# One PSUM pool of eight banks, and attention scores taken 512 keys at a time, in a fused sketch-attention and expert-attention kernel

## The chip, the core and the metric

The kernel runs on one core of a Trainium2 chip. The metric is device time in microseconds, the median of several executions. A core has a matrix engine (TensorE, PE in the profile; its weight loads are a row of their own, PEld), a vector engine (VectorE, DVE), an activation engine (ScalarE, ACT), a general one (GpSimd, POOL) and a queue for transfers (SyncE, SP). Matrix products land in PSUM, here used as eight banks of 128 partitions by 512 fp32 values; VectorE or ScalarE read them out from there.

## What is computed

Two blocks, one after the other. The first is an attention with a polynomial sketch: queries and keys (4 batches, 4 heads, 1088 positions, 32 values) become 64 features each, and the output is a ratio of two products with sums over all keys. Its output x, 1088 by 128 for each batch, goes through four "experts", each an ordinary causal attention of width 64; a gate picks two of four experts for each position. In short (cut):

```
for e in range(E):
    q = x @ wq[e]; k = x @ wk[e]; v = x @ wv[e]
    scores = scale * (q @ k.transpose(0, 2, 1))
    scores = np.where(causal, -1000000000.0, scores)
    scores = scores - scores.max(-1, keepdims=True)
    a = np.exp(scores)
    a /= a.sum(-1, keepdims=True) + 1e-09
    ye = a @ v @ wo[e]
    for kk in range(K):
        mask = topk[:, :, kk] == e
        out += mask[..., None] * w[:, :, kk:kk + 1] * ye
```

The change concerns the path from scores to a.

## The kernel before, in words

**Tiling.** Queries and keys are cut into tiles of 128 positions: i or j = 0 to 7, and a last tile of 64 (i = 8). Experts go in two groups g of two (e = 0, 1); the two sit in partitions 0 to 63 and 64 to 127 of qk and are multiplied side by side. Since the attention is causal, query tile i needs n = 128 i + 128 keys.

**The steps for one query tile and group.** `scores` (line 400) multiplies qk by qk into a tile sc (line 412), at most 512 keys an instruction. `soften` (393) lets VectorE add the mask, negate, store into an SBUF tile a, and keep the running minimum of the negated scores in mx (395); this is called a *take* below. ScalarE then computes the exponential of a in place with mx as bias and sums it into z (398). `turns_of` (469) transposes a on TensorE, tile by tile, into tp (477), which `evacuate` (67) copies into aT: every third copy goes to VectorE (70), the others to ScalarE (72). `values` (546) multiplies aT by v into av (552). `gates` (494) makes the weight rb from z (497 to 501); TensorE transposes it into the second half of the av tile (507), ScalarE copies it (509), and VectorE multiplies av by it into yT (557). That product empties the bank of av. `output` (614) multiplies yT by wo into po, which is copied and stored.

`scores_first` (421) does query tiles 0 and 1 together, `scores_last` (441) the last 64 queries of both groups: first the 64 diagonal keys into two tiles ext, then 1024 keys into sc. There VectorE takes ext first (through 395), then the 1024 keys in one instruction (464) that has the minimum of the ext take as its starting value, so the minimum of both comes out in mx; one exponential over all 1088 follows (466).

**PSUM.** Two pools. ps_sc (56) has two slots of two banks: an sc tile of 1024 keys of one expert, or of two experts by 512. ps_tp (57) has four slots of one bank for everything else: tp, av, po, ext, and the tiles of `prepare` (206), which makes qk, v and the gates of the next batch (kps and qps, the sketch; tq, num, tx, qk, vg). A tile may be written when the last reader of the bank's previous tile is done; such waits are put in when the program is built. Which slot a tile gets is also decided then.

**Order.** TensorE's instructions run in the order in which they are written (the block from 627 on). For each unit of work: `make` the scores of one query tile; multiply the values of groups that are ready; for a unit of kind G make the scores of the second query tile; then a row of jobs, transposes of the scores made before, mixed by `spend` (518) with pieces of `prepare` for the next batch (queued in `fill`). A batch has eight units: Q (tiles 0, 1), two of kind P (tiles 2, 3), four of kind G (tiles 4 to 7), L (the last 64). In the last batch there is no next one to prepare; units are split into kinds A and B. The other engines work in the order in which their instructions were scheduled at build time. Loads of the next batch are issued on SP in `begin_rest` (236), stores in `output` (624).

Of the kernel before, what the change touches and what calls it, by code (L numbers as in the profile page):

```python
# [10 lines left out]
F32 = mybir.dt.float32  # L11
BF16 = mybir.dt.bfloat16
I32 = mybir.dt.int32
ALU = mybir.AluOpType
ACTF = mybir.ActivationFunctionType
# [4 lines left out]
def kernel(  # L20
# [20 lines left out]
    nc = tc.nc  # L41
    B, H, S, D = q.shape
# [7 lines left out]
    NG = E // 2  # L50
    scale = 1.0 / math.sqrt(HD)
# [1 line left out]
    cp = ctx.enter_context(tc.tile_pool(name="const", bufs=1))  # L53
    p2 = ctx.enter_context(tc.tile_pool(name="p2", bufs=2))
    p4 = ctx.enter_context(tc.tile_pool(name="p4", bufs=4))
    ps_sc = ctx.enter_context(tc.tile_pool(name="ps_sc", bufs=2, space=bass.MemoryType.PSUM))
    ps_tp = ctx.enter_context(tc.tile_pool(name="ps_tp", bufs=4, space=bass.MemoryType.PSUM))

    def const(name, shape, dt=F32):
        return cp.tile(shape, dt, name=name, tag=name)  # L60
# [6 lines left out]
    def evacuate(out_, in_):  # L67
        turn[0] += 1
        if turn[0] % 3 == 0:
            nc.vector.tensor_copy(out_, in_)  # L70
        else:
            nc.scalar.copy(out_, in_)  # L72


    kin = const("kin", [128, S])
# [41 lines left out]
    with tc.issue_after(landing.ins):  # L117
        for x, w in enumerate((wq, wk)):
            nc.sync.dma_start(out=wqk[:, x], in_=w.rearrange("e p d -> p e d"))
        nc.sync.dma_start(  # L120
            out=wvg[:, 0 : E * HD].rearrange("p (e d) -> p e d", e=E), in_=wv.rearrange("e p d -> p e d"))
# [63 lines left out]
    mask = const("mask", [128, 1024], BF16)  # L185
# [20 lines left out]
    def prepare(b):  # L206
# [4 lines left out]
        gw = p2.tile([128, NJ, E], F32, tag="gw", name=f"gw{b}")  # L211
        gw8 = p2.tile([128, 2], F32, tag="gw8", name=f"gw8{b}")
        n = NJ - 1

        def bank(name):
            return ps_tp.tile([128, 512], F32, tag="tp", name=name)

        abS = {}
        fps = {}
# [170 lines left out]
        return (qk, vt, gw, gw8), ahead, mid, late  # L390


    def soften(a, src, msk, mx, z, most=3e38):

        nc.vector.tensor_tensor_reduce(out=a, in0=src, in1=msk, scale=-1.0, scalar=most,  # L395
                                       op0=ALU.add, op1=ALU.min, accum_out=mx)
        if z is not None:
            nc.scalar.activation(out=a, in_=a, func=ACTF.Exp, bias=mx, scale=-1.0, accum_out=z)  # L398

    def scores(b, i, g, qk, z):  # L400

        n = 128 * i + 128
        if n <= 512:
            t = ps_sc.tile([128, 2, 512], F32, tag="sc", name=f"sc{b}_{i}_{g}")
            sc = [t[:, e, :] for e in range(2)]
        else:
            sc = [ps_sc.tile([128, 1024], F32, tag="sc", name=f"sc{b}_{i}_{g}_{e}") for e in range(2)]
        for c0 in range(0, n, 512):
            c1 = min(c0 + 512, n)
            for e in range(2):  # L410
                rows = slice(64 * e, 64 * e + 64)
                nc.tensor.matmul(sc[e][:, c0:c1], qk[rows, g, 128 * i : 128 * i + 128], qk[rows, NG + g, c0:c1],  # L412
                                 start=True, stop=True)
        mx = p4.tile([128, 2], F32, tag="mx", name=f"mx{b}_{i}_{g}")
        width, tag, bufs = (512, "as", 8) if n <= 512 else (S, "a", 4)
        ats = [p4.tile([128, width], F32, tag=tag, name=f"a{b}_{i}_{g}_{e}", bufs=bufs) for e in range(2)]
        for e in range(2):
            soften(ats[e][:, 0:n], sc[e][:, 0:n], mask[:, 1024 - n :], mx[:, e : e + 1], z[:, e : e + 1])
        return ats

    def scores_first(b, qk, zs):

        made = [[[], []] for _ in range(NG)]
        for g in range(NG):
            t = ps_sc.tile([128, 2, 512], F32, tag="sc", name=f"sc{b}_0_{g}")
            for i in range(2):
                for e in range(2):
                    rows = slice(64 * e, 64 * e + 64)
                    nc.tensor.matmul(t[:, e, 128 * i : 256 * i + 128], qk[rows, g, 128 * i : 128 * i + 128],  # L429
                                     qk[rows, NG + g, 0 : 128 * i + 128], start=True, stop=True)  # L430
            mx = p4.tile([128, 2, 2], F32, tag="mx0", name=f"mx{b}_0_{g}")
            a = [p4.tile([128, 512], F32, tag="as", name=f"a{b}_0_{g}_{e}", bufs=8) for e in range(2)]
            for i in range(2):
                for e in range(2):
                    n, dst = 128 * i + 128, a[e][:, 128 * i : 256 * i + 128]
                    soften(dst, t[:, e, 128 * i : 256 * i + 128], mask[:, 1024 - n :], mx[:, i, e : e + 1],
                           zs[g][:, i, e : e + 1])
                    made[g][i].append(dst)
        return made

    def scores_last(b, qk, z):

        sc = [ps_sc.tile([128, 1024], F32, tag="sc", name=f"sc{b}_8_{e}") for e in range(2)]
        ext = [ps_tp.tile([128, 512], F32, tag="tp", name=f"ext{b}_{e}")[:, 0:64] for e in range(2)]

        def some(dst, e, c0, c1):
            rows = slice(64 * e, 64 * e + 64)
            for g in range(NG):
                nc.tensor.matmul(dst[64 * g : 64 * g + 64], qk[rows, g, 1024:], qk[rows, NG + g, c0:c1],  # L449
                                 start=True, stop=True)  # L450

        for e in range(2):
            some(ext[e], e, 1024, S)
        for c in range(0, 1024, 512):
            for e in range(2):
                some(sc[e][:, c : c + 512], e, c, c + 512)
        mx = p4.tile([128, 4], F32, tag="mx8", name=f"mx{b}_8")
        ats = [p4.tile([128, S], F32, tag="a", name=f"a{b}_8_{e}") for e in range(2)]
        for e in range(2):
            soften(ats[e][:, 1024:], ext[e], mask_last, mx[:, 2 + e : 3 + e], None)  # L460
        for e in range(2):

            most = mx[:, e : e + 1]
            nc.vector.tensor_tensor_reduce(out=ats[e][:, 0:1024], in0=sc[e], in1=mask[:, 0:1].to_broadcast([128, 1024]), scale=-1.0,
                                           scalar=mx[:, 2 + e : 3 + e], op0=ALU.add, op1=ALU.min, accum_out=most)
            nc.scalar.activation(out=ats[e], in_=ats[e], func=ACTF.Exp, bias=most, scale=-1.0, accum_out=z[:, e : e + 1])
        return ats

    def turns_of(name, i, ats, aT, q0):

        def some(e0, e1, j0, j1):
            tp = ps_tp.tile([128, 512], F32, tag="tp", name=f"tp{name}_{e0}_{j0}")
            nk, nj = size(j0), j1 - j0
            for e in range(e0, e1):
                for j in range(j0, j1):
                    x = 128 * (nj * (e - e0) + j - j0)
                    nc.tensor.transpose(tp[0:nk, x : x + 128], ats[e][:, 128 * j : 128 * j + nk], ident)  # L477
            evacuate(aT[0:nk, e0:e1, j0:j1, q0 : q0 + 128],
                     tp[0:nk, 0 : 128 * nj * (e1 - e0)].rearrange("p (e j s) -> p e j s", e=e1 - e0, j=nj))

        n = min(i + 1, NJ - 1)
        if n <= 2:
            cuts = [(0, 2, 0, n)]
        elif n <= 4:
            cuts = [(0, 1, 0, n), (1, 2, 0, n)]
        elif n <= 6:
            cuts = [(0, 1, 0, 4), (0, 2, 4, n), (1, 2, 0, 4)]
        else:
            cuts = [(0, 1, 0, 4), (0, 1, 4, n), (1, 2, 0, 4), (1, 2, 4, n)]
        if i == NJ - 1:  # L490
            cuts.append((0, 2, n, NJ))
        return [lambda c=c: some(*c) for c in cuts]
# [36 lines left out]
    def units(b, qk, vt, gw, gw8):  # L529
# [5 lines left out]
        for p in range((NJ - 1) // 2) if b < B - 1 else (1, 3, 2, 0):  # L535
# [3 lines left out]
            for g in range(NG):  # L539
# [4 lines left out]
                name = f"{b}_{p}_{g}"  # L544

                def values(p=p, g=g, aT=aT, yT=yT, name=name):
                    av = ps_tp.tile([128, 512], F32, tag="tp", name=f"av{name}")
                    for j in range(2 * p + 2):
                        lo = 128 * max(0, j - 2 * p)
                        for e in range(2):  # L550
                            c = HD * (2 * g + e)
                            nc.tensor.matmul(av[HD * e : HD * e + HD, lo:256], vt[:, j, c : c + HD],  # L552
                                             aT[:, e, j, lo:256], start=(j == 0), stop=(j == 2 * p + 1))

                    def finish(to_gate):
                        rs = to_gate(av[:, 256:])
                        nc.vector.tensor_tensor(out=yT[:, g], in0=av[:, 0:256], in1=rs, op=ALU.mult)  # L557
                        return [lambda: output(b, p, yT)] if g == NG - 1 else []

                    return finish  # L560
# [26 lines left out]
    def last_unit(b, qk, vt, gw8):  # L587
# [3 lines left out]
        yT = p2.tile([128, NG, 256], F32, tag="yT", name=f"yT{b}_8")  # L591

        def values():
            av = ps_tp.tile([128, 512], F32, tag="tp", name=f"av{b}_8")
            for g in range(NG):
                for j in range(NJ):
                    m = size(j)
# [15 lines left out]

    def output(b, p, yT):
        nq, n = (128, 2) if p < NJ // 2 else (64, 1)
        po = ps_tp.tile([128, 512], F32, tag="tp", name=f"po{b}_{p}")
        for x in range(n):
            for g in range(NG):
                nc.tensor.matmul(po[0:nq, DM * x : DM * x + DM], yT[:, g, 128 * x : 128 * x + nq], wo_sb[:, g],  # L619
# [6 lines left out]

    with tc.manual_schedule(engines={mybir.EngineType.PE}):

        warm = ps_tp.tile([128, 512], F32, tag="tp", name="warm")
        for _ in range(16):  # L630
            nc.tensor.matmul(warm[:, 0:128], idle, idle, start=True, stop=True)
        now, ahead, _, own = prepare(0)
# [103 lines left out]
```

## Time and profile before

The median of 3 runs is 398.3 us (398.27 to 398.81). The profiled execution took 398.61 us by the device's count, and its span in the profile is 396.8 us. The granted clock of TensorE is 1.0 of full speed all through.

| what | us or share | where it is read |
|---|---|---|
| span | 396.8 | top of the page |
| GpSimd busy | 58.7 (15%) | engine row |
| score matmuls, lines 412 / 429 / 449 | 320 / 64 / 64 records | groups of one tile |
| takes of scores (line 395) | 90.2 us, 128 times | costliest groups |
| exponentials (line 398) | 98.1 us, 128 times | costliest groups |
| transposes of a (line 477) | 90.1 us, 648 records | costliest groups |
| wait of takes for score matmuls | 62.1 us, 33 times | waits |
| wait of exponentials for takes | 59.2 us, 38 times | waits |
| chain that ended last: PE / DVE / ACT | 72% / 15% / 9% | chain of waits |

One fp32 matmul leaves two records. A row of the costliest groups gives the line, the engine and its operation, output<-input by name and shape, the count, busy time and mean, and behind the bar the idle time of the engine before these instructions and what ended it. Busy time of TensorE includes the modelled ends of pipelined matmuls. An idle time of VectorE or ScalarE costs nothing unless TensorE waits for what comes behind it.

### The profile page before, as it was taken

Reading aid. Unit: us, or ns where it says so; the run is one execution under the profiler, and the core shown is the slowest. Engines: PE = TensorE matmul, PEld = TensorE weight load, DVE = VectorE, ACT = ScalarE, POOL = GpSimd, SP = SyncE. Lnnn points to the kernel's source line nnn. Section 1 sums busy time; section 2 is a strip of 40 time slices with the busy share of each in tenths; the row PEclk is TensorE's granted clock in tenths of the full one; section 3 lists DMA queues with packets and bytes.
Section 4 is the critical chain, followed back from the end, with each engine's and each line's share of the span. In section 5 each row is a group of like instructions: output and inputs, shape, how many; then the busy total and the mean of one; then the engine's idle time right before and its main releaser. Section 6 shows DMA issues by size and latency. Waiting matters only on the chain.

```text
span 396.8 us, 8017 instructions
## 1 busy us (share of the span) xinstructions
PE 373.2 (94%) x3152; PEld 265.4 (67%) x3152; DVE 234.6 (59%) x661; ACT 226.5 (57%) x550; POOL 58.7 (15%) x87
## 2 busy tenths in 40 slices
PE   8898999999999999999999999999999999999995
PEld 7764687667665776767664767766756475666673
DVE  6867866555548675366456564555655844745551
ACT  2236666555666656456475656754665565656582
POOL 3400461000001740000000541000000010000010
PEclk9999999999999999999999999999999999999999
DMA  7705022000000000000000000000000000000000
GB/s 192 200 2 170 16 98 71 2 1 15 13 2 0 15 2 5 15 0 15 1 15 0 2 13 7 13 2 0 15 13 2 1 16 6 0 15 2 15 4 26
DMA packets 11349, 9.95 MB, mean 25 GB/s; under 512 B 3632, under 2 KB 10288, under 8 KB 11312
## 3 DMA queue, kind: packets, MB, share of 16 engines
q1 hardware_dynamic: 11296, 9.44, 8.6%
q8 instruction: 24, 0.39, 0.4%
q14 instruction: 13, 0.11, 0.1%
q10 hardware_dynamic: 16, 0.00, 0.0%
HBM read 7.22 MB, written 2.23 MB: 24 GB/s over the span
## 4 chain that ended last, share of the span: by engine, by line
PE 72%; DVE 15%; ACT 9%; issue 2%; DMA 2%; SPq 0%; ACTq 0%; DVEq 0%
PE av L552 16%; PE sc L412 15%; PE tp L477 14%; DVE a L395 7%; ACT a L398 7%; PE qk L326 5%; PE vg L338 3%; PE num L300 3%; PE po L619 3%; PE av L600 3%; PE sc L449 2%; DMA qin<-in_q_dram 2%; DVE qT L223 1%; PE sc L429 1%; PE qps L251 1%
## 5 line engine op out<-in xcount | busy, mean ns | idle before, releaser
L398 ACT ACTIVATE a<-a,mx 128x256 f32<-128x256 f32 (+7 forms) x128 | 98.1, 767 | 59.6 <-DVE mx L395 59.2
L395 DVE CUSTOM_DVE_ANT_0 a<-sc,mask 128x256 f32<-128x256 f32 (+7 forms) x128 | 90.2, 754 | 64.1 <-PE sc L412 62.1
L477 PE MATMUL tp<-ident,a 128*128 128x128 f32 (+1 forms) x648 | 90.1, 276 | 10.6 <-DVE yT L557 6.8
L477 PEld LDWEIGHTS tp<-ident,a 128*128 128x128 f32 (+1 forms) x648 | 72.8, 142 | 26.0 <-DVE yT L557 10.2
L72 ACT COPY aT<-tp 128x512 f32<-128x512 f32 (+3 forms) x119 | 61.6, 544 | 17.9 <-PE tp L477 17.2
L552 PE MATMUL av<-aT,vt 128*64 128x256 f32 (+1 forms) x640 | 67.9, 362 | 0.0
L412 PE MATMUL sc<-qkT 64*128 64x512 f32 (+3 forms) x320 | 67.7, 541 | 0.0
L501 POOL TENSOR_TENSOR rb<-gw,r 128x256 f32<-128x256 f32 (+1 forms) x36 | 21.1, 589 | 297.2 <-DVE r L498 227.2
L552 PEld LDWEIGHTS av<-aT,vt 128*64 128x64 f32 x640 | 43.2, 137 | 31.0 <-issue 10.0
L70 DVE COPY aT<-tp 128x512 f32<-128x512 f32 (+3 forms) x61 | 38.6, 633 | 21.4 <-PE tp L477 21.3
L412 PEld LDWEIGHTS sc<-qkT 64*128 64x128 f32 x320 | 27.9, 186 | 23.7 <-issue 19.9
L326 PE MATMUL qk<-xT,wqk 128*128 128x512 f32 x64 | 31.1, 602 | 0.0
L509 ACT COPY rs<-av 128x256 f32<-128x256 f32 (+1 forms) x36 | 12.1, 356 | 27.7 <-PE av L507 27.6
L398 ACT ACTIVATION_READ_ACCUMULATOR a<-a,mx 128x1 f32 x128 | 23.9, 187 | 0.0
L619 PE MATMUL po<-wo,yT 128*128 128x128 f32 (+1 forms) x144 | 20.4, 281 | 1.7 <-DVE yT L557 1.5
L338 PE MATMUL vg<-wvg,xT 128*128 128x260 f32 (+1 forms) x72 | 20.2, 392 | 1.5 <-DVE vt L70 1.5
L497 DVE TENSOR_SCALAR r<-z 128x4 f32<-128x4 f32 (+1 forms) x36 | 6.3, 176 | 23.5 <-ACT a L398 16.6
L72 ACT COPY qkT<-qk 128x512 f32<-128x512 f32 x20 | 11.7, 585 | 14.4 <-PE qk L326 14.1
L619 PEld LDWEIGHTS po<-wo,yT 128*128 128x128 f32 (+1 forms) x144 | 17.3, 185 | 3.5 <-DVE yT L557 1.9
L300 PE MATMUL num<-kvz,qpT 128*128 128x66 f32 x144 | 17.9, 273 | 0.2 <-ACT qpT L72 0.2
L300 PEld LDWEIGHTS num<-kvz,qpT 128*128 128x128 f32 x144 | 17.1, 192 | 0.9 <-ACT qpT L72 0.5
L326 PEld LDWEIGHTS qk<-xT,wqk 128*128 128x128 f32 x64 | 10.7, 190 | 8.4 <-issue 4.7
(118 smaller groups left out, 392.0 us busy)
## 6 DMA issues: line engine op xcount, KB each, us to landing
kin<-in_k_dram SPq DMA_DIRECT2D x4, 544.0 KB, 4.0
qin<-in_q_dram SPq DMA_DIRECT2D x4, 544.0 KB, 5.1
vin<-in_v_dram SPq DMA_DIRECT2D x16, 128.0 KB, 5.7
out_dram<-ob SPq DMA_DIRECT2D x16, 128.0 KB, 1.8
vtl<-in_v_dram SPq DMA_DIRECT2D x8, 16.0 KB, 3.4
wqk<-in_moe_wq_dram SPq DMA_DIRECT2D x1, 128.0 KB, 5.3
wqk<-in_moe_wk_dram SPq DMA_DIRECT2D x1, 128.0 KB, 3.2
wvg<-in_moe_wv_dram SPq DMA_DIRECT2D x1, 128.0 KB, 3.1
```

The source lines that it names most:

```text
L70: nc.vector.tensor_copy(out_, in_)
L72: nc.scalar.copy(out_, in_)
L300: nc.tensor.matmul(num[:, 66 * (y - 2 * x0) : 66 * (y - 2 * x0) + 66], qpT[:, y], kvz[:, y % 2].rearrange("p h d -> p (h d)"), start=True, ...
L326: nc.tensor.matmul(t, wt(a), xT[:, 512 * c : 512 * c + 512], start=True, stop=True)
L338: nc.tensor.matmul(t[0:m, 0 : E * HD + E], xT[:, 128 * j : 128 * j + m], wvg, start=True, stop=True)
L395: nc.vector.tensor_tensor_reduce(out=a, in0=src, in1=msk, scale=-1.0, scalar=most, op0=ALU.add, op1=ALU.min, accum_out=mx)
L398: nc.scalar.activation(out=a, in_=a, func=ACTF.Exp, bias=mx, scale=-1.0, accum_out=z)
L412: nc.tensor.matmul(sc[e][:, c0:c1], qk[rows, g, 128 * i : 128 * i + 128], qk[rows, NG + g, c0:c1], start=True, stop=True)
L477: nc.tensor.transpose(tp[0:nk, x : x + 128], ats[e][:, 128 * j : 128 * j + nk], ident)
L501: nc.gpsimd.tensor_tensor(out=rb[:, 0 : w // 128].rearrange("p x (e d) -> p x e d", d=HD), in0=gws[:, :, :, None].to_broadcast(wide), in1= ...
L552: nc.tensor.matmul(av[HD * e : HD * e + HD, lo:256], vt[:, j, c : c + HD], aT[:, e, j, lo:256], start=(j == 0), stop=(j == 2 * p + 1))
L619: nc.tensor.matmul(po[0:nq, DM * x : DM * x + DM], yT[:, g, 128 * x : 128 * x + nq], wo_sb[:, g], start=(g == 0), stop=(g == NG - 1))
```

## The change

The two pools become one, ps, with eight slots of one bank under one tag; `bank` gives out a tile of 512 columns. Every PSUM tile of the kernel comes from it. `soften` is cut in two: `take` (VectorE) and `soften` (the exponential). In `scores` the keys go 512 at a time: for each piece two banks, one for each expert, two matmuls, then two takes; the second piece starts from the minimum of the first, and the exponential over all keys follows the last piece. Keys stay in the order in which they were multiplied. `scores_first` uses a bank for each expert. `scores_last` goes through 512, 512 and 64 keys, so the diagonal keys, which were first, come last.

```
-    ps_sc = ctx.enter_context(tc.tile_pool(name="ps_sc", bufs=2, space=bass.MemoryType.PSUM))
-    ps_tp = ctx.enter_context(tc.tile_pool(name="ps_tp", bufs=4, space=bass.MemoryType.PSUM))
+    ps = ctx.enter_context(tc.tile_pool(name="ps", bufs=8, space=bass.MemoryType.PSUM))
...
+    def bank(name):
+        return ps.tile([128, 512], F32, tag="bank", name=name)
...
-    def soften(a, src, msk, mx, z, most=3e38):
-
-        nc.vector.tensor_tensor_reduce(out=a, in0=src, in1=msk, scale=-1.0, scalar=most,
+    def take(dst, src, msk, mx, most=3e38):
+
+        nc.vector.tensor_tensor_reduce(out=dst, in0=src, in1=msk, scale=-1.0, scalar=most,
                                        op0=ALU.add, op1=ALU.min, accum_out=mx)
-        if z is not None:
-            nc.scalar.activation(out=a, in_=a, func=ACTF.Exp, bias=mx, scale=-1.0, accum_out=z)
+
+    def soften(a, mx, z):
+
+        nc.scalar.activation(out=a, in_=a, func=ACTF.Exp, bias=mx, scale=-1.0, accum_out=z)
 
     def scores(b, i, g, qk, z):
 
         n = 128 * i + 128
-        if n <= 512:
-            t = ps_sc.tile([128, 2, 512], F32, tag="sc", name=f"sc{b}_{i}_{g}")
-            sc = [t[:, e, :] for e in range(2)]
-        else:
-            sc = [ps_sc.tile([128, 1024], F32, tag="sc", name=f"sc{b}_{i}_{g}_{e}") for e in range(2)]
-        for c0 in range(0, n, 512):
-            c1 = min(c0 + 512, n)
+        mx = p4.tile([128, 2, 2], F32, tag="mx", name=f"mx{b}_{i}_{g}")
+        width, tag, bufs = (512, "as", 8) if n <= 512 else (S, "a", 4)
+        ats = [p4.tile([128, width], F32, tag=tag, name=f"a{b}_{i}_{g}_{e}", bufs=bufs) for e in range(2)]
+        for c in range(0, n, 512):
+            keys = slice(c, min(c + 512, n))
+            sc = [bank(f"sc{b}_{i}_{g}_{c}_{e}")[:, 0 : keys.stop - c] for e in range(2)]
             for e in range(2):
                 rows = slice(64 * e, 64 * e + 64)
-                nc.tensor.matmul(sc[e][:, c0:c1], qk[rows, g, 128 * i : 128 * i + 128], qk[rows, NG + g, c0:c1],
+                nc.tensor.matmul(sc[e], qk[rows, g, 128 * i : 128 * i + 128], qk[rows, NG + g, keys],
                                  start=True, stop=True)
-        mx = p4.tile([128, 2], F32, tag="mx", name=f"mx{b}_{i}_{g}")
-        width, tag, bufs = (512, "as", 8) if n <= 512 else (S, "a", 4)
-        ats = [p4.tile([128, width], F32, tag=tag, name=f"a{b}_{i}_{g}_{e}", bufs=bufs) for e in range(2)]
-        for e in range(2):
-            soften(ats[e][:, 0:n], sc[e][:, 0:n], mask[:, 1024 - n :], mx[:, e : e + 1], z[:, e : e + 1])
+            for e in range(2):
+                m = mx[:, e, c // 512 : c // 512 + 1]
+                take(ats[e][:, keys], sc[e], mask[:, 1024 - n + c : 1024 - n + keys.stop], m,
+                     mx[:, e, 0:1] if c else 3e38)
+                if keys.stop == n:
+                    soften(ats[e][:, 0:n], m, z[:, e : e + 1])
         return ats
 
     def scores_first(b, qk, zs):
 
         made = [[[], []] for _ in range(NG)]
         for g in range(NG):
-            t = ps_sc.tile([128, 2, 512], F32, tag="sc", name=f"sc{b}_0_{g}")
+            sc = [bank(f"sc{b}_0_{g}_{e}") for e in range(2)]
             for i in range(2):
                 for e in range(2):
                     rows = slice(64 * e, 64 * e + 64)
-                    nc.tensor.matmul(t[:, e, 128 * i : 256 * i + 128], qk[rows, g, 128 * i : 128 * i + 128],
+                    nc.tensor.matmul(sc[e][:, 128 * i : 256 * i + 128], qk[rows, g, 128 * i : 128 * i + 128],
                                      qk[rows, NG + g, 0 : 128 * i + 128], start=True, stop=True)
             mx = p4.tile([128, 2, 2], F32, tag="mx0", name=f"mx{b}_0_{g}")
             a = [p4.tile([128, 512], F32, tag="as", name=f"a{b}_0_{g}_{e}", bufs=8) for e in range(2)]
             for i in range(2):
                 for e in range(2):
-                    n, dst = 128 * i + 128, a[e][:, 128 * i : 256 * i + 128]
-                    soften(dst, t[:, e, 128 * i : 256 * i + 128], mask[:, 1024 - n :], mx[:, i, e : e + 1],
-                           zs[g][:, i, e : e + 1])
-                    made[g][i].append(dst)
+                    n, cols = 128 * i + 128, slice(128 * i, 256 * i + 128)
+                    m = mx[:, i, e : e + 1]
+                    take(a[e][:, cols], sc[e][:, cols], mask[:, 1024 - n :], m)
+                    soften(a[e][:, cols], m, zs[g][:, i, e : e + 1])
+                    made[g][i].append(a[e][:, cols])
         return made
 
     def scores_last(b, qk, z):
 
-        sc = [ps_sc.tile([128, 1024], F32, tag="sc", name=f"sc{b}_8_{e}") for e in range(2)]
-        ext = [ps_tp.tile([128, 512], F32, tag="tp", name=f"ext{b}_{e}")[:, 0:64] for e in range(2)]
-
-        def some(dst, e, c0, c1):
-            rows = slice(64 * e, 64 * e + 64)
-            for g in range(NG):
-                nc.tensor.matmul(dst[64 * g : 64 * g + 64], qk[rows, g, 1024:], qk[rows, NG + g, c0:c1],
-                                 start=True, stop=True)
-
-        for e in range(2):
-            some(ext[e], e, 1024, S)
-        for c in range(0, 1024, 512):
+        mx = p4.tile([128, 2, 3], F32, tag="mx8", name=f"mx{b}_8")
+        ats = [p4.tile([128, S], F32, tag="a", name=f"a{b}_8_{e}") for e in range(2)]
+        for c in range(3):
+            keys = slice(512 * c, min(512 * c + 512, S))
+            sc = [bank(f"sc{b}_8_{c}_{e}")[:, 0 : keys.stop - 512 * c] for e in range(2)]
             for e in range(2):
-                some(sc[e][:, c : c + 512], e, c, c + 512)
-        mx = p4.tile([128, 4], F32, tag="mx8", name=f"mx{b}_8")
-        ats = [p4.tile([128, S], F32, tag="a", name=f"a{b}_8_{e}") for e in range(2)]
-        for e in range(2):
-            soften(ats[e][:, 1024:], ext[e], mask_last, mx[:, 2 + e : 3 + e], None)
-        for e in range(2):
-
-            most = mx[:, e : e + 1]
-            nc.vector.tensor_tensor_reduce(out=ats[e][:, 0:1024], in0=sc[e], in1=mask[:, 0:1].to_broadcast([128, 1024]), scale=-1.0,
-                                           scalar=mx[:, 2 + e : 3 + e], op0=ALU.add, op1=ALU.min, accum_out=most)
-            nc.scalar.activation(out=ats[e], in_=ats[e], func=ACTF.Exp, bias=most, scale=-1.0, accum_out=z[:, e : e + 1])
+                rows = slice(64 * e, 64 * e + 64)
+                for g in range(NG):
+                    nc.tensor.matmul(sc[e][64 * g : 64 * g + 64], qk[rows, g, 1024:], qk[rows, NG + g, keys],
+                                     start=True, stop=True)
+            for e in range(2):
+
+                m = mx[:, e, c : c + 1]
+                take(ats[e][:, keys], sc[e], mask[:, 0:512] if c < 2 else mask_last, m,
+                     mx[:, e, c - 1 : c] if c else 3e38)
+                if c == 2:
+                    soften(ats[e], m, z[:, e : e + 1])
         return ats
 
-            tp = ps_tp.tile([128, 512], F32, tag="tp", name=f"tp{name}_{e0}_{j0}")
+            tp = bank(f"tp{name}_{e0}_{j0}")
...
```

The other uses of ps_tp (in `prepare`, `values`, `last_unit`, `output` and for the warm-up) become calls of `bank` in the same way.

More of the change, by code (lines that the diff above doesn't have):

```diff
@@ L213, in prepare @@
         n = NJ - 1
-        def bank(name):
-            return ps_tp.tile([128, 512], F32, tag="tp", name=name)
         abS = {}
@@ L546, in values @@
                 def values(p=p, g=g, aT=aT, yT=yT, name=name):
-                    av = ps_tp.tile([128, 512], F32, tag="tp", name=f"av{name}")
+                    av = bank(f"av{name}")
                     for j in range(2 * p + 2):
@@ L593, in values @@
         def values():
-            av = ps_tp.tile([128, 512], F32, tag="tp", name=f"av{b}_8")
+            av = bank(f"av{b}_8")
             for g in range(NG):
@@ L615, in output @@
         nq, n = (128, 2) if p < NJ // 2 else (64, 1)
-        po = ps_tp.tile([128, 512], F32, tag="tp", name=f"po{b}_{p}")
+        po = bank(f"po{b}_{p}")
         for x in range(n):
@@ L627 @@
     with tc.manual_schedule(engines={mybir.EngineType.PE}):
-        warm = ps_tp.tile([128, 512], F32, tag="tp", name="warm")
+        warm = bank("warm")
         for _ in range(16):
```

## The prediction

> **What bounds the kernel now.** I read the page's first part, then the list of waits, once for TensorE's matmuls and once for its weight loads, then the timeline of one unit of work.
>
> ```profile
> PE 373.2 (94%) x3152; PEld 265.4 (67%) x3152; DVE 234.6 (59%) x661; ACT 226.5 (57%) x550; POOL 58.7 (15%) x87
> ```
>
> TensorE (PE) sets the time: 396.8 - 373.2 leaves it 23.6 us without a matmul, while VectorE (DVE) has 162 us idle and ScalarE (ACT) 170. TensorE's order is written by hand, so whatever stalls one of its instructions moves everything behind it. The waits of the weight loads (PEld) say what stalls it:
>
> ```profile
> PEld sc L412 <- issue: 19.9, 94, 0.2
> PEld tp L477 <- DVE yT L557: 10.2, 12, 1.2
> ...
> PEld tp L477 <- ACT aT L72: 3.1, 5, 1.1
> PEld kps L251 <- ACT aT L72: 2.7, 4, 1.1
> PEld vg L338 <- DVE vt L70: 2.3, 2, 1.2
> PEld tp L477 <- DVE aT L70: 2.3, 4, 0.8
> ```
>
> The columns are total us, times, longest. "issue" is the ordinary cadence of a score's weight load. The others share a form: a transpose waits for a product (yT) of which it reads nothing, a sketch matmul (kps) for the copy of a transpose. Only a PSUM bank links these pairs: the instruction named is the reader that empties the bank which the waiting one overwrites. One such place, in the timeline (start us, length us, then in brackets the idle time before):
>
> ```profile
> 167.79 1.56 PE L412 MATMUL sc<-qkT 64*128 64x512 f32 x8
> ...
> 169.38 0.96 DVE L395 CUSTOM_DVE_ANT_0 a<-sc,mask 128x768 f32<-128x768 f32 x1 [3.96 <-PE sc L412]
> ...
> 169.77 0.60 PE L477 MATMUL tp<-ident,a 128*128 128x128 f32 x4
> ...
> 170.21 0.60 PE L290 MATMUL tq<-ident,qp 128*128 128x128 f32 x4
> 170.26 0.08 DVE L395 DVE_READ_ACCUMULATOR2_ANT mx<- 128x1 f32 x1
> 170.26 0.95 DVE L395 CUSTOM_DVE_ANT_0 a<-sc,mask 128x768 f32<-128x768 f32 x1
> 170.44 0.94 ACT L398 ACTIVATE a<-a,mx 128x768 f32<-128x768 f32 x1
> ...
> 171.14 0.75 DVE L557 TENSOR_TENSOR yT<-av,rs 128x256 f32<-128x256 f32 x2
> ...
> 171.61 0.44 PE L477 MATMUL tp<-ident,a 128*128 128x128 f32 x2 [0.81 <-DVE yT L557]
> ```
>
> The four banks of ps_tp hold av of two groups, tp and tq; the next tp is a fifth tile. The av banks are emptied by yT, and yT stands in VectorE's queue behind both takes of the new scores. TensorE stands still for 0.81 us by the matmul row and 1.04 by the weight-load row.
>
> **How much stall is there?** I add all gaps of this kind. By matmul rows: yT 6.8 (11 times), kps 1.6, vg 1.5, and smaller ones (tp behind aT, ob, xT; tx; the transposes behind xs) 3.8: 13.7 us. By weight-load rows: 23.9 us in 32 gaps, less 0.17 us each that such a load idles without any wait (the 0.17 ahead of scores at 162.46): 18.5. Here a rule of the Trainium skill decides which row to trust ("Perfetto Trace Analysis", Identifying the Most-Contended Engine): matmul busy time is a bad measure of headroom, since pipelined matmuls blur it, and weight-load occupancy is better. By the first the stall is 13.7, by the rule 18.5 (raw occupancy, 33% idle, would promise far more, but most of that is the cadence above). I take the middle, 16 us.
>
> **The change, part by part.**
>
> *One pool of eight.* Nothing is added; the four score banks join the other four. At 170.57, when the tp above wants a bank (171.61 - 1.04), eight are taken: av twice, tp, tq, four of scores. But now the scores give theirs back one by one. How soon: VectorE starts 1.37, 1.59, 1.81 and 2.02 us after the first score matmul for 640, 768, 896 and 1024 keys (162.47 to 163.84, 167.79 to 169.38, 175.64 to 177.45, 179.87 to 181.89), 0.217 per 128 keys; so for the first 512 alone 1.15 (estimate). That take would run from 168.94 to 169.63, and the bank is there 0.9 us early. The stall goes. The same count works for the 1.18 us gaps at 105.97, 200.50 and 294.92 (av, po, tx, vg and then tp).
> What is late next: the transposes of the newer scores, at 174.21, come some 0.9 us earlier, 173.3; their exponentials end at 172.3 in the old trace. Covered.
>
> *Takes by 512 keys.* Scores of 640 to 1024 keys (16 tiles a batch, 64 in all) take two instructions for one; the last query tile three for two (8 tiles). 72 more. From the rows: 128x512 takes 688 ns, 128x1024 1222, a slope of 134 per 128 keys; back to back they pace at 0.61 and 1.145 us (229.69 to 230.30; 183.04 to 184.19), so one more start costs 0.08. The later chunk reads its bound from mx: the row of the last tile with such an operand is 1282 against 1222, 0.06 more. 72 x 0.14 = 10 us of VectorE. The Trainium skill speaks against this in the same page (Optimizing Scalar/DVE Operations): each VectorE access to PSUM has some 125 ns of overhead, and grouping into larger operations helps a saturated engine. By that rule the change costs 72 x 0.125 = 9 us, an estimate, on the path if VectorE were the bound. The trace has it idle 162 us, so I put none of it on the path as throughput. As latency it counts. Per unit of two heads, with the earlier start: the end of the takes moves by +0.06, -0.17, -0.37, -0.60 us (640, 768, 896, 1024: start earlier by 0.22, 0.43, 0.65, 0.87, work longer by 0.27). The first exponential now waits for three takes and not one: for 640 keys 0.61 + 0.61 + 0.28 (0.22 for 128 keys, and the 0.06) against 0.75, less 0.22 of earlier start: +0.53; in the same way 768 +0.31; 896 +0.10; 1024 -0.12. In the first three batches nothing is due that early (slack 0.7 us or more, above). In the last batch, where little other work is left, TensorE waits for exponentials already (0.50 at 345.82, 0.33 at 374.66): two units of 640 and two of 768 there cost 2 x 0.53 + 2 x 0.31 = 1.7 us.
>
> *The last query tile.* Its 64 diagonal keys come last and not first. Takes 2 x 0.61 + 2 x 0.67 + 0.21 from about 208.1 put the first exponential near 211.0, against 210.53: 0.5 us later. Ahead of its users TensorE has vg and 3.6 us of qk; without that cover it would cost 0.5 x 4 = 2 us. I count 0. It holds six banks, as before.
>
> *scores_first and short tiles.* Same instructions, banks of their own: 0. TensorE's instruction count, SyncE's and GpSimd's queues and all DMAs stay.
>
> *The added wait.* Scores never waited for a bank: the idle time before their matmuls is 0.0 in the row of L412. Now they compete with tiles that ACT empties, behind exponentials. Bounds: none, if a free bank is always found (at 190.62 three tp are pending, 3 + 4 below 8); at the other end 60 score groups (15 units of banks a batch, four batches) at 0.43 us, the mean of today's bank waits (13.7 / 32), 26 us. The timeline's counts stand near the lower end: I take 2.
>
> **Sum.** 16 less 1.6 that I leave in the last batch (gaps at 333.53, 341.04, 343.34, where copies sit behind exponentials), less 1.7, less 2: 10.7. From the profiled run, 398.6 (span 396.8 and 1.8 around it), 387.9; the median of the plain runs is 0.3 lower. I say 388, own range 383 to 392.
>
> **Rivals.**
> 1. *Half is given back.* TensorE no longer stalls for banks but arrives early where copies of aT and exponentials are due; ACT, with 7 to 9 of 14 us busy per unit, drains in bursts. For: several gaps (223.16, 333.53) end with an ACT copy queued behind exponentials. Against: the slack of 0.7 us after the stall is gone. Half of 10.7 is left: 393.3.
> 2. *Slower: scores wait.* A tile that empties late (av until yT, tp behind two exponentials of 1.15 us) sits in the bank that the next score is to use, TensorE stops, and the takes, exponentials and transposes start late with it. Without new waits the gain is 12.7; over 60 groups it is used up at 0.21 us each. At 0.28, 17 us: 398.6 - 12.7 + 17 = 403. For: banks are assigned when the program is built, in an expected order of release, and one pool lets a slow tenant reach the scores. Against: in the old trace vg at 201.00 takes the bank freed at 200.78, not the older one of po freed at 201.7, so the assignment follows releases well.
> 3. *Nothing happens:* the stalls are replaced by equal ones at the same transposes, bounded by exponentials. 398. The slack above speaks against it.
>
> **How the numbers follow.** Forecast 0.58, half back 0.19, slower 0.17, nothing 0.06. A measurement of this kernel tells about 0.2% from no change (0.8 us), so faster 0.76, same 0.06, slower 0.18. Range: down to 382.5, where all 16 us return; up to 399.5, which takes in the first rival and the mild end of the second and leaves out some 15 in 100 above and 4 below.
>
> **What would show it.** Right: waits of tp for yT fall from 10.2 us to under 3, kps and vg waits vanish, VectorE's busy time is about 245 us, TensorE's idle share drops to some 3%. Takes start 0.2 to 0.9 us sooner after the scores. The forecast is wrong if idle time appears ahead of score matmuls (second rival), or if transposes wait for exponentials in the first three batches (first and third).

## The result, and the profile after

The changed kernel takes 378.38 us (median of 4 runs, 378.13 to 381.03), the kernel before 398.28 (398.19 to 398.81): a ratio of 0.951, 95% interval 0.947 to 0.956. Direction and mechanism were as forecast; the size was not. The gain is about 20 us, where 10.7 were forecast, and the time lies below the stated range of 383 to 392. The profiled execution has a span of 376.5 us, 20.3 less.

The engine line, the chain by engine and the row of the score matmuls, from the changed kernel's page:

```profile
PE 366.5 (97%) x3152; PEld 267.7 (71%) x3152; DVE 241.0 (64%) x805; ACT 221.2 (59%) x550; POOL 58.6 (16%) x87
...
PE 86%; DVE 5%; ACT 3%; issue 2%; DMA 2%; SPq 0%; ACTq 0%; DVEq 0%
...
L412 PE MATMUL sc<-qkT 64*128 64x512 f32 (+3 forms) x320 | 67.6, 541 | 0.0
```

TensorE does the same 3152 records in 20 us less. VectorE has 144 records more: 72 takes and 72 reads of their minimum. The chain through VectorE and ScalarE shrank from 24% to 8%. The last number of the third line, idle time ahead of score matmuls, is still 0.0: scores do not wait for the shared banks. Nor does the first matmul of any unit of scores start later after the record before it than in the old trace (48 units, all within 0.001 us).

What is left of the waits of weight loads (us in total, times, longest) for transposes tp. The first is a wait for data, the second what remains of waits for yT:

```profile
PEld tp L472 <- ACT a L399: 1.9, 2, 1.1
...
PEld tp L472 <- DVE yT L600: 0.5, 2, 0.2
```

And the place that the prediction showed, in the changed kernel's timeline:

```profile
157.74 1.56 PE L412 MATMUL sc<-qkT 64*128 64x512 f32 x8
158.90 0.69 DVE L394 CUSTOM_DVE_ANT_0 a<-sc,mask 128x512 f32<-128x512 f32 x1 [3.47 <-PE sc L412]
...
160.16 0.60 PE L289 MATMUL tq<-ident,qp 128*128 128x128 f32 x4
...
160.60 0.38 PE L472 MATMUL tp<-ident,a 128*128 128x128 f32 x2
...
160.71 0.94 ACT L399 ACTIVATE a<-a,mx 128x768 f32<-128x768 f32 x1 [0.63 <-DVE mx L394]
...
160.94 0.42 DVE L552 TENSOR_TENSOR yT<-av,rs 128x256 f32<-128x256 f32 x1
```

VectorE starts 1.16 us after the first score matmul, where it was 1.59 (estimated: 1.15). The two transposes at 160.60 follow tq in 0.44 us; before it was 1.40. They start before yT, which they used to wait for.

Where did the 20.3 us come from? TensorE's order is the same in both traces, apart from the 64 diagonal keys of the last tile. So the stretches between the same score matmuls can be compared (us, rounded one by one; score matmuls of lines 412 and 429, now 430, are the marks):

| stretch, before | length before | after | difference |
|---|---|---|---|
| 0 to 28.1, first sketch | 28.1 | 27.8 | -0.4 |
| 28.1 to 40.6, vg and qk of batch 0 | 12.5 | 10.5 | -2.0 |
| 40.6 to 122.9, batch 0 | 82.3 | 76.9 | -5.4 |
| 122.9 to 217.4, batch 1 | 94.6 | 89.3 | -5.3 |
| 217.4 to 311.8, batch 2 | 94.3 | 89.3 | -5.0 |
| 311.8 to 396.8, batch 3 | 85.0 | 82.9 | -2.2 |

The same can be done matmul by matmul. I compared, in the two traces, the time from the start of each record to the start of the next (a count of my own, not a view of the page). Some entries:

```
waiting matmul, start before   start to start: before -> after
vg   32.59                     1.13 -> 0.22
tp   62.96                     1.08 -> 0.11
tp  105.98                     1.15 -> 0.22
tp  171.61                     1.08 -> 0.11
kps 223.16                     1.10 -> 0.11
tp  333.53                     1.17 -> 0.11
tp  374.66                     0.60 -> 1.13
kv   14.29                     0.41 -> 0.93
```

Gaps that shrank by more than 0.12 us come to 22.9 us, those that grew to 4.8; 3.0 of both are only the new order within the last tile, four times. That leaves 19.9 of stalls gone, 1.9 of new ones, and 2.2 of many smaller changes: 20.2, the span's difference within rounding.

Not all of this is banks. Of the 19.9, 1.7 us lie in the first 13.1 us, at waits that the prediction did not count, and there they are mostly lost again: ten warm-up matmuls more start 0.21 us apart in place of 0.11 (28 of 31 such steps, 18 before; a second trace of the changed kernel has 19, so this varies between runs), and kv waits 0.52 longer. The first stretch gains only 0.4. Behind it, 18.2 us of stalls are gone at 28 places, 1.3 are new, and smaller changes bring 3.1. Of these, 1.8 belong to the stalls: at each of the 28 places the record right behind the waiting one also starts 0.03 to 0.10 sooner after it than before. So the stalls that went had cost 20.0 us; 1.2 stay unexplained.

### The profile page after: what moved, and what is told of

The parts are those of the page before. It is cut to its first block, busy times and chain, and to the rows that moved or that the text cites. A ratio compares the mean times of both kernels' runs of the same rounds, so it can differ in the third digit from the quotient of the medians.

```text
span 376.5 us, 8233 instructions
## 1 busy us (share of the span) xinstructions
PE 366.5 (97%) x3152; PEld 267.7 (71%) x3152; DVE 241.0 (64%) x805; ACT 221.2 (59%) x550; POOL 58.6 (16%) x87
## 4 chain that ended last, share of the span: by engine, by line
PE 86%; DVE 5%; ACT 3%; issue 2%; DMA 2%; SPq 0%; ACTq 0%; DVEq 0%
PE tp L472 18%; PE av L547 17%; PE sc L412 16%; PE qk L325 8%; PE num L299 4%; PE po L614 3%; PE vg L337 3%; PE av L595 3%; PE av L502 3%; ACT a L399 3%; PE sc L453 2%; PE tq L289 2%; PE sc L430 2%; DMA qin<-in_q_dram 2%; PE kv L276 2%
## 5 line engine op out<-in xcount | busy, mean ns | idle before, releaser
L399 ACT ACTIVATE a<-a,mx 128x256 f32<-128x256 f32 (+8 forms) x136 | 107.5, 791 | 92.1 <-DVE mx L394 92.1
L394 DVE CUSTOM_DVE_ANT_0 a<-sc,mask 128x512 f32<-128x512 f32 (+3 forms) x136 | 74.2, 593 | 46.5 <-PE sc L412 42.4
L472 PE MATMUL tp<-ident,a 128*128 128x128 f32 (+1 forms) x648 | 87.5, 274 | 1.8 <-ACT a L399 1.5
L472 PEld LDWEIGHTS tp<-ident,a 128*128 128x128 f32 (+1 forms) x648 | 73.8, 142 | 12.1 <-issue 4.2
L547 PEld LDWEIGHTS av<-aT,vt 128*64 128x64 f32 x640 | 43.2, 137 | 28.1 <-issue 6.8
L412 PEld LDWEIGHTS sc<-qkT 64*128 64x128 f32 x320 | 27.7, 186 | 23.8 <-issue 17.6
L394 DVE CUSTOM_DVE_ANT_0 a<-sc,mask,mx 128x512 f32<-128x512 f32 (+3 forms) x72 | 38.3, 570 | 0.0
L399 ACT ACTIVATION_READ_ACCUMULATOR a<-a,mx 128x1 f32 x136 | 25.4, 187 | 0.0
L504 ACT COPY rs<-av 128x256 f32<-128x256 f32 (+1 forms) x36 | 12.2, 349 | 12.9 <-PE av L502 12.9
L394 DVE DVE_READ_ACCUMULATOR2_ANT mx<- 128x1 f32 x216 | 18.1, 84 | 0.0
```

What stands on the lines that cost most here:

```text
L394: nc.vector.tensor_tensor_reduce(out=dst, in0=src, in1=msk, scale=-1.0, scalar=most, op0=ALU.add, op1=ALU.min, accum_out=mx)
L412: nc.tensor.matmul(sc[e], qk[rows, g, 128 * i : 128 * i + 128], qk[rows, NG + g, keys], start=True, stop=True)
```

## The experiments

Two theories stood at the start. A: the gain is the sharing of the banks. B: the gain is the early start of the takes, which brings yT, and with it the bank of av, forward. All times are medians beside runs of the kernel before on the same chip (398.6 to 398.7 us).

**Two pools, takes by 512 keys.** Scores keep four banks of their own, now single ones; all else has four (the 64 diagonal keys of the last tile too, as before the change).

```
-    ps = ctx.enter_context(tc.tile_pool(name="ps", bufs=8, ...))
+    ps_sc = ctx.enter_context(tc.tile_pool(name="ps_sc", bufs=4, ...))
+    ps = ctx.enter_context(tc.tile_pool(name="ps", bufs=4, ...))
...
-            sc = [bank(f"sc{b}_{i}_{g}_{c}_{e}")[:, 0 : keys.stop - c] for e in range(2)]
+            sc = [sc_bank(f"sc{b}_{i}_{g}_{c}_{e}")[:, 0 : keys.stop - c] for e in range(2)]
```

> Takes by 512 keys as in the changed kernel, but scores in a pool of four single banks of their own and everything else in four banks, as before the change (the 64 diagonal keys of the last tile too). Theory A (shared banks give the gain): the stalls of the transposes behind yT stay, shortened only by what the takes end earlier (0.17 to 0.60 us at 768 to 1024 keys): 392 to 396 us. Theory B (the earlier start of the takes gives it, because yT and with it the av bank come earlier): 379 to 384 us.

407.5 us, ratio 1.022 (1.020 to 1.024): *slower* than before, by 9 us. B's forecast fails, and A did not expect a loss either. The timeline of the unit with 1024 keys, first before, then in this run, shows it:

```profile
181.79 0.44 PE L507 MATMUL av<-ident,rb 128*128 128x128 f32 x2
...
182.32 0.37 ACT L509 COPY rs<-av 128x256 f32<-128x256 f32 x1 [1.52 <-PE av L507]
...
183.22 1.15 ACT L398 ACTIVATE a<-a,mx 128x1024 f32<-128x1024 f32 x1 [0.53 <-DVE mx L395]
...
184.19 0.42 DVE L557 TENSOR_TENSOR yT<-av,rs 128x256 f32<-128x256 f32 x1
```

```profile
184.08 0.44 PE L506 MATMUL av<-ident,rb 128*128 128x128 f32 x2
...
185.40 1.15 ACT L403 ACTIVATE a<-a,mx 128x1024 f32<-128x1024 f32 x1 [2.21 <-DVE mx L398]
...
186.55 1.13 ACT L403 ACTIVATE a<-a,mx 128x1024 f32<-128x1024 f32 x1
...
187.68 0.35 ACT L508 COPY rs<-av 128x256 f32<-128x256 f32 x1
187.93 0.37 ACT L72 COPY ob<-po 128x256 f32<-128x256 f32 x1
...
188.36 0.44 PE L293 MATMUL tq<-ident,qp 128*128 128x128 f32 x2 [1.21 <-ACT ob L72]
188.43 0.41 DVE L556 TENSOR_TENSOR yT<-av,rs 128x256 f32<-128x256 f32 x1
```

Before, ScalarE copied rs 0.5 us after the start of the gate's transposes, ahead of the two exponentials, though the program writes it after them. Now it copies rs 3.6 us after, behind both, and yT, which empties av, comes 4.35 us after the gate in place of 2.40. Nothing in the change speaks of this: ScalarE's order is made when the program is built. In the program of this run, and of the changed kernel too, nine of the 36 copies of rs stand behind two more exponentials than before. With four banks TensorE pays for it: at 188.36 it waits 1.21 us for the copy of po (ob).

This is theory C: the loss of this run comes from the order on ScalarE, which holds banks for longer. Against it D: the loss is the extra work of VectorE.

**The last piece taken first.** In `scores` all matmuls come first, then the takes, beginning with the last piece, so that VectorE cannot start before all keys are multiplied; `scores_first` and `scores_last` as in the changed kernel.

```
+        for c in reversed(tiles):
+            keys, sc = tiles[c]
...
+                     mx[:, e, 1:2] if c == 0 and n > 512 else 3e38)
+                if c == 0:
+                    soften(ats[e][:, 0:n], m, z[:, e : e + 1])
```

With one pool of eight:

> One pool of eight, but in the tiles of 256 to 1024 keys the takes begin with the last piece, so VectorE cannot start before all score matmuls of the pair are done, as before the change. Theory A (shared banks): 378 to 382 us, at most some later exponentials in the last batch. Theory B (early start): most of the gain is lost, 388 us or more.

377.66 us, ratio 0.948 (0.946 to 0.951). VectorE starts 1.38, 1.59, 1.80 and 2.02 us after the first score matmul for 640, 768, 896 and 1024 keys, as before the change, and the whole gain is there. The early start is not needed for it: B is refuted, A holds.

With two pools of four:

> The kernel with two pools of four single banks and takes by 512 keys, but with the last piece taken first. Theory C (in the two-pool run the loss of 9 us comes from ScalarE's order: the copies of rs were placed behind both exponentials there, so yT and with it the av banks come late; with the late start of the takes the program has rs ahead of them again in all those places): 397 to 400 us, about the kernel before. Theory D (the loss comes from VectorE's extra instructions, which delay yT by 0.3 us a unit): 405 us or more, since these stay and the takes even end later.

400.9 us, ratio 1.006 (1.005 to 1.008). The extra instructions are all there, VectorE's busy time is 245.4 us (244.0 in the run above), and 6.6 of the 8.8 us are gone. D is refuted. The order is back, in the same unit:

```profile
181.19 0.44 PE L510 MATMUL av<-ident,rb 128*128 128x128 f32 x2
...
181.72 0.37 ACT L512 COPY rs<-av 128x256 f32<-128x256 f32 x1 [1.01 <-PE av L510]
...
182.88 1.15 ACT L403 ACTIVATE a<-a,mx 128x1024 f32<-128x1024 f32 x1 [0.79 <-DVE mx L398]
...
183.31 0.42 DVE L560 TENSOR_TENSOR yT<-av,rs 128x256 f32<-128x256 f32 x1
...
184.09 0.38 PE L293 MATMUL tq<-ident,qp 128*128 128x128 f32 x2
```

rs is again copied 0.5 us after the gate and tq does not wait. One reservation: VectorE's order changed too (yT now stands ahead of the last take), so this shows that the order of the two engines makes the loss, not how much of it is ScalarE's share. A hint: from start to start, 12.2 us of TensorE's stalls are longer in the run above than in this one (changes over 0.12 us), and 8.7 of them end, by the profile, with a copy by ScalarE.

**Fewer banks in the shared pool.** Only the number in `bufs` is changed.

```
-    ps = ctx.enter_context(tc.tile_pool(name="ps", bufs=8, ...))
+    ps = ctx.enter_context(tc.tile_pool(name="ps", bufs=7, ...))
```

> The changed kernel with seven banks in place of eight. Theory A: with one spare bank fewer a part of the stalls is back, 380 to 386 us. Theory B: 378 to 380, the starts of the takes do not change. A third reading, that the eighth bank is never needed, gives 378.4.

383.5 us (382.0 to 387.0), ratio 0.963 (0.958 to 0.968). In the profiled run, 387.0 us, TensorE's granted clock was 0.89 and 0.77 in the first two stretches of 20 us; the two runs with a mean clock of 1.00, 382.0 and 382.5 us, are the better figure for the bank. Stalls return at the same jobs: vg at 106.96, 197.22 and 287.48 come 0.7 us later after the record before them than with eight.

> The changed kernel with six banks. Theory A: scores and transposes both stall, 388 to 402 us, and idle time appears ahead of score matmuls. Theory B: 379 to 384, what comes from waits of scores alone.

389.25 us (387.6 to 390.3), ratio 0.975 (0.972 to 0.977); the two runs with a mean clock of 1.00 took 387.6 and 388.8. The bank waits grow, for instance at vg, which waits for the copy of po that ScalarE makes behind the exponentials and rs:

```profile
196.62 0.35 ACT L504 COPY rs<-av 128x256 f32<-128x256 f32 x1
196.87 0.37 ACT L71 COPY ob<-po 128x256 f32<-128x256 f32 x1
...
197.29 1.14 PE L337 MATMUL vg<-wvg,xT 128*128 128x260 f32 x4 [0.97 <-ACT ob L71]
```

Scores, which A expected to wait here, do so once: at 332.73 a weight load of theirs sits idle 0.46 us until a copy of aT is done.

Each bank taken away costs something: some 4 us for the eighth, some 6 for the seventh. B, for which the number of banks hardly mattered, falls here too. Yet *six shared banks are 9 us faster than the eight of the kernel before*.

> One shared pool of six banks with the last piece taken first. Theory C (ScalarE's order holds banks for long): with rs ahead of the exponentials the six banks turn round sooner, 382 to 386 us against 389.3 with the early takes. Theory D (only the count of banks matters and the takes' start is worth little): 389 to 391.

383.54 us, ratio 0.963 (0.961 to 0.964). With the other order the same six banks are worth 5.7 us more (4 to 5 against the two runs at full clock), as C said.

**VectorE's extra work made larger.** Takes of at most 256 keys in `scores` for tiles of 384 keys and more.

```
-                take(ats[e][:, keys], sc[e], ...)
+                for k in range(c, keys.stop, 256):
+                    k1, y = min(k + 256, keys.stop), k // 256
...
+                    take(ats[e][:, k:k1], sc[e][:, k - c : k1 - c], ...)
```

> The changed kernel with takes of at most 256 keys in the tiles of 384 to 1024 keys: 128 more instructions, by 0.14 us each 18 us more VectorE work. If VectorE's work is hidden behind TensorE: 378 to 381 us. If the added instructions stand on the path (grouping rule): 390 us or more.

381.43 us, ratio 0.959 (0.956 to 0.962), 3.1 us above the changed kernel. Its engine line:

```profile
PE 366.2 (96%) x3152; PEld 267.8 (71%) x3152; DVE 268.7 (71%) x1061; ACT 221.9 (58%) x550; POOL 58.6 (15%) x87
```

VectorE works 27.7 us more, and 3.1 of them reach the end, slightly more than the reading "hidden" allowed. What shows is latency: the transposes at 328.57, in the last batch, wait 1.06 us more for their exponential, those at 51.97 1.25 more for yT. The order of the copies of rs on ScalarE differs a little too, so the 3.1 are not VectorE's work alone. The grouping rule of the Trainium skill that the prediction weighed ("Perfetto Trace Analysis", Optimizing Scalar/DVE Operations) is for a saturated engine; at 71% busy, 27.7 us of added work cost 3.1.

**Experts one after the other.** Both pieces of the first expert are taken before those of the second.

```
+        for e in range(2):
+            for c, (keys, sc) in tiles.items():
...
+            soften(ats[e][:, 0:n], m, z[:, e : e + 1])
```

> The changed kernel with both pieces of the first expert taken before those of the second, so that its exponential starts up to 0.5 us earlier. If the stalls for exponentials that are left in the last batch (1.0 us there in all) follow from the order of the takes: 377.4 to 378.1 us. If a take whose bound was written by the instruction just before it has to wait for that write, or ScalarE has other work first: 378.4 or more.

378.64 us, ratio 0.950 (0.949 to 0.952): no change, but neither reading was tested. In the trace the orders of TensorE, VectorE and ScalarE are those of the changed kernel to the last instruction; only the text of the program was different.

**The faster of two.**

> The changed kernel once more, beside the next one on the same chip: 378.4 us.

> One pool of eight with the last piece taken first, once more, to tell its 377.7 us from the changed kernel's 378.4 on one chip. If rs ahead of the exponentials is still worth something with eight banks: 0.5 to 1.0 us below the changed kernel. If eight banks hide ScalarE's order entirely: equal within 0.3 us.

378.23 us, ratio 0.951 (0.948 to 0.953), and 377.73, 0.947 (0.946 to 0.949). The version that takes the last piece first was the lower one both times, by 0.5 to 0.7 us. The intervals of the ratios just touch, so this is likely and not certain. The traces fit it. Three of the changed kernel's new stalls, 0.25 to 0.31 us each, are transposes that wait for copies which ScalarE makes behind both exponentials and rs, for instance

```profile
189.99 0.42 PEld L472 LDWEIGHTS tp<-ident,a 128*128 128x128 f32 x4 [0.50 <-ACT ob L71]
```

and with the last piece first all three are gone, 0.8 us. It is the fastest version found.

All in one table (us):

| banks | scores by 1024 | by 512, first piece first | by 512, last piece first |
|---|---|---|---|
| 4 + 4 | 398.6 | 407.5 | 400.9 |
| 6 shared | | 387.6 to 389.3 | 383.5 |
| 7 shared | | 382.0 to 383.5 | |
| 8 shared | | 378.2 to 378.4 | 377.7 |

Down the columns: with the same takes, sharing all eight is worth 29 and 23 us. Within each column the orders of TensorE and ScalarE are the same in the traces of four and four and of eight; VectorE's differs in a few places. Along the first row: taking by 512 keys, without sharing, costs 2 to 9 us. It earns its place only by making the score tiles one bank large, so that they fit into a common pool. Wide takes in a shared pool were not tried: a take across two banks needs a pair of neighbours, which a pool of single banks does not give.

## Why the prediction was right and wrong

**Right: what bounds the kernel and what the waits are.** The stalls named were bank waits, and they went. Waits of tp for yT fell from 10.2 to 0.5 us, those of kps for copies of aT from 2.7 to 0.2 and those of vg for vt from 2.3 to nothing, VectorE's busy time is 241 us (245 forecast), TensorE's idle share 3%. The bank was there in time where the count said so.

**Wrong: the sum of stalls, 16 us.** Two terms of the sum failed, and this is the first: it was mis-sized. The bank stalls that went had cost 20.0 us, 18.2 at the waiting records and 1.8 at those right behind. I had taken the middle between matmul rows (13.7) and weight-load rows (18.5). The Trainium skill's rule ("Perfetto Trace Analysis", Identifying the Most-Contended Engine) pointed the right way: the weight-load sum was close to the 18.2, the matmul rows were far off. But single rows of both kinds under-tell. At 171.61 the matmul row says 0.81 us, the weight-load row 1.04 less 0.17 = 0.87; from start to start the gap was 1.08 where 0.11 is usual: 0.97 lost. A matmul's modelled end reaches into its stall, by 0.16 here, and gaps shorter than that do not show as idle time at all.

**Wrong: the charges against it, 5.3 us.** This is the second term that failed. For scores that wait for banks I took 2 us: there were none (0.0 ahead of them). 1.6 was left standing in the last batch: at 333.53 and 341.04 the gaps went to the usual 0.11, and at 343.34 no matmul had waited. For later exponentials in the last batch I took 1.7: one place paid, the transpose at 374.66, by +0.53, exactly the 0.53 worked out for 640 keys; the other units had cover. The 0 for the last tile's later exponential held: nothing behind it waits longer. New stalls for copies, three of 0.25 to 0.31, come to 0.8. So 1.3 was lost where 5.3 had been charged.

Of the 9.6 us by which the gain was under-told, 4.0 belong to the stalls (20.0 - 16) and 4.0 to the charges (5.3 - 1.3); 0.4 came in the first stretch, and 1.2 are the small changes that stay unexplained. The lower end of the range, "where all 16 us return", fell with the first.

**Right in size: VectorE's extra work.** With their reads, the takes keep VectorE busy 112.0 us in place of 102.1: 9.9 for 72 more, or 0.14 each, where 10 was worked out. The estimate of 9 from the Trainium skill's 125 ns ("Perfetto Trace Analysis", Optimizing Scalar/DVE Operations) was close too. One figure in the working mixes two counts: the mean bank wait of 0.43 us divides the 13.7 us of the matmul rows by the 32 gaps of the weight-load rows. The matmul rows have 25 gaps, which makes 0.55, and the upper bound for waits of scores 33 us in place of 26; the forecast did not rest on it.

**Not foreseen: ScalarE's order.** The prediction took the other engines' orders as given. They are made anew when the program is built, and here rs moved behind the exponentials in nine places. With eight shared banks the version that undoes this is 0.5 to 0.7 us faster, with four and four 6.6; some of that may be VectorE's order.

**The rivals.** Half given back: no; copies kept up but for 0.8 us. Scores wait: no, as the 0.0 shows; but its worry, a slow tenant that holds a bank, is what six banks show, at vg above all and only once at scores. Nothing happens: no.

## What to carry to other kernels

Buffers split between two uses by a fixed count can be worth less than fewer in common: here six shared banks beat four and four with the same takes by 17 to 18 us. Size a stall by the time from start to start of the waiting engine's instructions against its usual cadence, the next record included, and not by idle rows that modelled ends have shortened. And when an edit changes when something becomes ready, compare the built order of *every* engine before and after: a copy that frees a buffer can slip behind long instructions on an engine whose own instructions are the same.

## What the runs showed beyond that

The cost of a take depends on what stands before it. The changed kernel's 72 more cost 0.14 us each, the 128 narrower ones of 256 keys 0.22 (27.7 us in all). In that trace a take that needs the minimum of the take right before it starts 0.12 us after the read of that minimum (172.01 to 172.13); the next take, of the other expert, starts together with the read before it (172.54).

TensorE's clock, 1.0 in every stretch of the kernel before, was granted at 0.77 to 0.92 between 20 and 40 us in the profiles of the runs with seven and six banks, and those runs spread by 5.0 and 2.7 us. Single runs of the other versions had it too: the changed kernel's 381.03 us has a mean clock of 0.990, its other three 0.999. What brought it about, no run here shows.
